# A hand-ordered attention-plus-FFN kernel: a new instruction order, new PSUM banks and a reshuffled head of loads

## The chip, the cores and the metric

The kernel runs on one core of a Trainium2 chip. The core has a matrix engine (PE, whose weight loads are profiled apart as PEld), a vector engine (DVE), a scalar engine (ACT), GpSimd (POOL) and a sync engine (SP). Each engine works through its own instruction stream strictly in order and waits on semaphores. Here POOL issues nearly all loads, SP issues the transposing DMAs and the stores, and all of these share the core's 16 DMA engines. The metric is device time in microseconds for one execution, as a median of several runs.

## The reference

What is computed, cut to its core: a linear attention with an exponential feature map, followed by a two-layer feed-forward network (FFN) with a squared ReLU.

```python
# q, k, v: (8, 8, 576, 64); w_phi: (64, 128); w_in: (512, 2048); w_out: (2048, 512)
def phi(x):
    proj = np.einsum('bhsd,df->bhsf', x, w_phi)
    proj = proj - np.max(np.abs(proj), axis=-1, keepdims=True)
    return np.concatenate([np.exp(proj), np.exp(-proj)], axis=-1)
q_p, k_p = (phi(q), phi(k))
kv = np.einsum('bhsf,bhsd->bhfd', k_p, v)
z = np.sum(k_p, axis=2)
num = np.einsum('bhsf,bhfd->bhsd', q_p, kv)
den = np.einsum('bhsf,bhf->bhs', q_p, z)[..., None] + 1e-06
attn = num / den                      # then (batch, seq, heads*64) -> x: (4608, 512)
h = np.maximum(x @ w_in, 0.0)
out = h * h @ w_out
```

## The kernel before

The eight batches are worked through one after another. The attention of batch b+1 is woven into the FFN of token chunk b, so that PE always has dense FFN matmuls between the small attention ones. A chunk is 512 tokens of one batch; the ninth chunk gathers the last 64 tokens of all eight batches (tile `xS`).

Nothing is scheduled while the program is built. A planner object (`Plan`) collects 1,680 numbered steps, each tied to one engine (some have an alternative engine). Then five tables at the end of the file decide everything. `ORDER` is the list of step numbers in the order in which they are emitted, and so the order on every engine, which `pin` fixes with explicit dependencies. `BASES` has one digit for each of 377 PSUM groups, its first bank (0 to 7); a group that takes a bank waits until the last users of that bank are done. `STATES` has one bit for each of 233 copy-like steps: its own engine or its alternative (DVE or ACT). `GATES` (lines 1061 to 1073) holds back each load of batches 2 and up until a given step is done. `FILL` names the PE steps ahead of which a number of dummy matmuls on the tile `warm` is put (line 961).

The steps and lines that the text below speaks of:

- Head, batch 0: steps 13 and 12 load parts of k (L249), 14 and 19 load q (L278), 26 loads k of batch 1. Txk and Txq (L320) transpose 128-token blocks on PE; Cxk and Cxq (L193 on DVE, L195 on ACT) copy them out of PSUM. Pk and Pq (L347, L491) project on w_phi, Mk and Mq (L386, L405, L498) take the maxima, and the exponentials are on ACT (L394, L411, L584). V (L428) scales v, KV (L462) and KVs (L450) build kv, NA and NB (L648, L599) multiply by it. SA (L660), rd (L670) and xo (L674, L618) finish the rows. Steps 119, 120, 126 and 127 turn the first rows round, and f1a 307 (L813) is the first FFN matmul group.
- From batch 2 on, k and q are transposed by DMA (Xxk and Xxq, L331, on SP's queue), for batch 2 as steps 373 and 374. From batch 1 on the finished rows xo are transposed by DMA into `xT` (Xx, L708): steps 266, 275, 284 and 293 for batch 1; 437, 446, 455 and 464 for batch 2. `xo` is a ring of three buffers, so xo 292 has to wait until Xx 266 has read its buffer. In batches 3 to 7 the features of q are also transposed by DMA (Xf, L548).
- FFN: F1 (L788; L799, L813 and L827 for the first chunk) needs all of a chunk's `xT`; relu (L765 on ACT, L767 on DVE) and sq (L774) make h; F2 (L882) and F2h (L846, the last tokens) multiply by w_out; ot (L193 or L195) copies the result out, and SP stores it.
- On POOL, 33, 34 and 35 load v of batch 1, 36 to 39 w_out, 22 to 25 w_in, and 355 to 358 the k of batch 2, of which 356 is gated by step 170 (Pq of batch 0).

Of the kernel before, what the change touches and what calls it, by code (L numbers as in the profile page):

```python
# [108 lines left out]
def kernel(  # L109
# [858 lines left out]
    2, 0, 1, 13, 14, 12, 8, 6, 7, 5, 3, 4, 11, 19, 40, 41, 9, 42, 46, 48, 10, 74, 66, 47, 75, 15, 67, 76, 45, 43, 18,  # L968
    68, 44, 77, 17, 71, 58, 88, 16, 90, 59, 70, 89, 26, 91, 27, 60, 78, 69, 92, 20, 49, 80, 81, 79, 28, 50, 61, 21,
    93, 51, 94, 30, 72, 52, 54, 98, 63, 57, 95, 22, 99, 64, 131, 65, 73, 53, 23, 55, 62, 83, 24, 156, 82, 132, 25,  # L970
    157, 29, 56, 133, 101, 38, 85, 128, 102, 84, 109, 86, 34, 212, 87, 110, 103, 213, 36, 111, 129, 214, 37, 112,
    104, 113, 105, 100, 215, 130, 33, 194, 158, 106, 195, 218, 108, 107, 216, 188, 219, 96, 114, 189, 121, 97, 115,
    134, 217, 122, 200, 206, 135, 116, 123, 207, 124, 159, 117, 125, 201, 136, 118, 126, 160, 190, 137, 127, 119,
    191, 120, 142, 161, 138, 145, 143, 220, 146, 307, 308, 221, 147, 139, 311, 312, 309, 144, 233, 162, 313, 303,
    140, 163, 304, 223, 148, 141, 164, 149, 322, 305, 222, 165, 310, 150, 166, 319, 323, 306, 151, 315, 314, 320,
    152, 196, 316, 198, 321, 167, 317, 153, 197, 325, 154, 199, 318, 328, 168, 326, 169, 155, 324, 170, 174, 329,
    208, 171, 356, 186, 175, 331, 330, 35, 187, 209, 176, 184, 39, 245, 332, 334, 246, 32, 185, 173, 177, 234, 31,
    172, 340, 335, 178, 361, 211, 327, 202, 359, 179, 203, 341, 477, 360, 210, 481, 365, 180, 181, 204, 357, 242,
    336, 346, 225, 243, 224, 355, 205, 485, 358, 247, 342, 347, 236, 363, 182, 267, 226, 276, 362, 268, 352, 183,
    235, 337, 269, 364, 227, 366, 192, 277, 489, 353, 549, 193, 338, 278, 237, 254, 238, 373, 255, 239, 490, 348,  # L980
    244, 248, 241, 258, 240, 249, 228, 259, 229, 230, 270, 260, 231, 374, 285, 333, 343, 271, 232, 339, 261, 344,
    272, 262, 495, 286, 263, 499, 250, 287, 264, 273, 265, 503, 274, 266, 354, 294, 251, 295, 507, 252, 275, 256,
    296, 279, 508, 513, 280, 253, 257, 551, 345, 288, 281, 547, 289, 349, 282, 556, 283, 290, 379, 350, 284, 375,
    553, 382, 517, 291, 376, 744, 531, 292, 377, 367, 381, 293, 297, 535, 370, 298, 378, 369, 380, 521, 552, 299,
    351, 422, 548, 387, 300, 423, 539, 389, 546, 525, 301, 557, 390, 371, 543, 526, 388, 554, 438, 544, 413, 550,
    482, 439, 414, 372, 486, 440, 563, 483, 416, 368, 424, 484, 383, 487, 429, 417, 747, 478, 430, 555, 564, 474,
    488, 431, 384, 740, 492, 475, 479, 476, 391, 504, 395, 392, 385, 500, 493, 404, 505, 518, 406, 501, 302, 494,
    396, 522, 386, 506, 502, 510, 397, 523, 527, 405, 565, 480, 415, 496, 394, 524, 519, 540, 497, 511, 393, 514,
    498, 398, 532, 491, 515, 407, 754, 545, 541, 516, 419, 559, 447, 533, 420, 399, 400, 749, 448, 401, 741, 534,
    408, 449, 582, 512, 739, 409, 403, 402, 410, 562, 583, 536, 411, 737, 421, 412, 432, 520, 585, 668, 561, 433,  # L990
    738, 537, 528, 418, 584, 742, 434, 672, 435, 748, 529, 436, 558, 574, 538, 437, 425, 456, 577, 542, 722, 746,
    426, 457, 560, 575, 726, 934, 428, 458, 441, 730, 442, 743, 576, 530, 443, 604, 444, 427, 734, 445, 607, 446,
    450, 605, 465, 676, 466, 755, 467, 451, 680, 606, 735, 452, 570, 681, 453, 566, 454, 704, 572, 567, 686, 608,
    609, 571, 568, 459, 569, 708, 745, 460, 573, 616, 461, 586, 455, 619, 690, 462, 463, 587, 468, 618, 712, 509,
    469, 464, 578, 617, 470, 580, 694, 620, 471, 472, 716, 581, 628, 579, 640, 631, 698, 736, 621, 589, 665, 630,
    756, 588, 683, 699, 629, 596, 666, 673, 595, 717, 677, 674, 682, 632, 667, 590, 678, 641, 591, 633, 592, 684,
    669, 593, 594, 935, 598, 701, 937, 670, 473, 597, 642, 687, 679, 931, 671, 675, 945, 610, 688, 695, 611, 643,
    689, 691, 752, 685, 696, 612, 943, 702, 705, 613, 692, 614, 750, 765, 703, 706, 599, 936, 652, 693, 600, 767,
    707, 723, 928, 697, 653, 768, 939, 719, 724, 932, 655, 766, 601, 720, 753, 713, 603, 938, 654, 602, 757, 769,
    714, 751, 758, 622, 645, 731, 658, 930, 623, 759, 859, 715, 933, 760, 732, 771, 624, 634, 656, 625, 709, 635,  # L1000
    626, 863, 710, 770, 644, 636, 727, 711, 877, 733, 728, 637, 638, 772, 867, 729, 718, 721, 700, 807, 725, 761,
    615, 881, 764, 885, 809, 639, 762, 871, 808, 947, 763, 889, 872, 646, 810, 895, 647, 890, 795, 773, 797, 627,
    648, 1128, 913, 649, 650, 929, 798, 899, 774, 651, 777, 917, 796, 786, 657, 811, 776, 659, 903, 660, 775, 921,
# [104 lines left out]
```

## Time and profile before

| what | us |
|---|---|
| median of 3 runs | 345.33 |
| lowest, highest | 344.21, 345.71 |
| the profiled execution, its own time | 346.37 |
| its span (first to last instruction) | 344.6 |
| lies around the span in that execution | 1.77 |

The page of the profile gives PE busy 97% of the span, DVE 78%, ACT 64% and POOL 28%. A busy PE counts a matmul from its start to its modelled end; these overlap, so a gap of PE shows only where it is longer than that overlap. Times in the rows that follow count from the start of the span. SPq and POOLq are the DMA queues that these engines issue. A row of a timeline has start, duration, engine, line, operation and tiles, how many instructions are merged, and in brackets the idle time ahead of it and what ended that.

### The profile page before, as it was taken

The numbers are of one execution on the slowest core, as the hardware profiler recorded it, in microseconds if no ns is written. First come the engines' busy times: TensorE is split into PE (matmuls) and PEld (weight loads), VectorE is DVE, ScalarE is ACT, GpSimd is POOL, SyncE is SP. The second block draws the span as 40 slices with busy tenths as digits, with TensorE's granted clock in tenths as the row PEclk, the third lists the DMA queues.
The fourth block names the chain that finished last, engine by engine and source line by source line (L and its number), as shares of the span: only waits on it lengthen the run. The fifth ranks groups of instructions, "written<-read, shape, count | busy, mean of one in ns | idle before, by whom it ended". The sixth has DMA issues, their size and how long they took to land.

```text
span 344.6 us, 8417 instructions
## 1 busy us (share of the span) xinstructions
PE 333.8 (97%) x3371; PEld 189.0 (55%) x3402; DVE 269.2 (78%) x490; ACT 221.6 (64%) x388; POOL 95.5 (28%) x143
## 2 busy tenths in 40 slices
PE   8999999799998999999999999999999999999995
PEld 7789776445554554545545554555555454444443
DVE  5999998799888798888869987798978748861540
ACT  5999996499898787577887896886376201111101
POOL 8760571952910480104604061330000000000000
PEclk9999999999999999999999999999999999999999
DMA  9999999999999999999999999999964631101115
GB/s 135 176 205 202 201 131 157 181 154 210 128 165 195 197 169 197 177 182 185 193 178 178 170 195 168 214 151 171 199 123 92 135 90 54 47 0 62 31 58 126
DMA packets 142935, 51.51 MB, mean 149 GB/s; under 512 B 111472, under 2 KB 138416, under 8 KB 142896
## 3 DMA queue, kind: packets, MB, share of 16 engines
q1 hardware_dynamic: 97488, 32.35, 51.8%
q0 software_dynamic: 44960, 18.23, 46.3%
q8 instruction: 26, 0.43, 0.6%
q10 hardware_dynamic: 448, 0.39, 0.4%
q14 instruction: 13, 0.11, 0.1%
HBM read 36.73 MB, written 9.44 MB: 134 GB/s over the span
## 4 chain that ended last, share of the span: by engine, by line
PE 86%; DVE 5%; DMA 5%; issue 2%; ACT 1%; POOL 1%; SPq 0%; DVEq 0%; POOLq 0%
PE psum L882 31%; PE psum L788 30%; PE psum L648 5%; PE psum L462 5%; PE psum L347 5%; DMA xT<-xo 3%; PE psum L827 2%; DMA kT<-xk 2%; DVE mk L405 2%; PE psum L813 1%; PE psum L799 1%; PE psum L569 1%; PE psum L846 1%; PE psum L320 1%; PE psum L450 1%
## 5 line engine op out<-in xcount | busy, mean ns | idle before, releaser
L882 PE MATMUL psum<-wout,h 128*128 128x512 bf16 x529 | 127.7, 379 | 1.7 <-issue 0.3
L788 PE MATMUL psum<-xT,win 128*128 128x512 bf16 x448 | 104.7, 379 | 1.0 <-DMA xT<-xo 1.0
L765 ACT ACTIVATE hr<-psum 128x512 bf16<-128x512 f32 x95 | 54.9, 601 | 47.9 <-DVE h L774 28.8
L882 PEld LDWEIGHTS <-h 128*128 128x128 bf16 x560 | 51.3, 98 | 56.7 <-issue 0.3
L788 PEld LDWEIGHTS <-win 128*128 128x128 bf16 x512 | 47.4, 98 | 53.6 <-DMA xT<-xo 1.4
L774 DVE TENSOR_TENSOR h<-hr 128x512 bf16<-128x512 bf16 x144 | 56.6, 415 | 10.6 <-ACT hr L765 10.2
L544 ACT ACTIVATE qf<-psum 128x1024 bf16<-128x1024 f32 (+1 forms) x50 | 45.6, 937 | 8.6 <-PE psum L347 6.1
L405 DVE TENSOR_REDUCE mk<-psum 128x8 f32<-128x1024 f32 (+1 forms) x38 | 42.3, 1119 | 4.0 <-ACT kn L411 1.9
L411 ACT ACTIVATE kn<-psum 128x1024 bf16<-128x1024 f32 (+1 forms) x38 | 36.0, 947 | 12.8 <-PE psum L347 11.1
L411 ACT ACTIVATE kp<-psum 128x1024 bf16<-128x1024 f32 (+1 forms) x38 | 35.6, 948 | 8.2 <-PE psum L347 6.6
L767 DVE TENSOR_SCALAR hr<-psum 128x512 bf16<-128x512 f32 x49 | 33.1, 684 | 9.0 <-PE psum L788 8.2
L660 DVE TENSOR_TENSOR psum<-psum,en 128x520 f32<-128x520 f32 (+1 forms) x39 | 27.2, 703 | 10.4 <-PE psum L648 6.1
L648 PEld LDWEIGHTS <-qpn 128*128 128x128 bf16 x624 | 27.0, 97 | 15.0 <-issue 3.3
L269 POOL DMA_DIRECT2D xq<-in_q_dram x24 | 17.3, 727 | 56.3 <-issue 14.0
L531 DVE TENSOR_REDUCE mq<-psum 128x8 f32<-128x1024 f32 (+1 forms) x25 | 27.8, 1113 | 6.5 <-PE psum L347 3.9
L648 PE MATMUL psum<-kv,qpn 128*128 128x65 bf16 x624 | 30.2, 193 | 1.9 <-DVE xo L674 1.7
L249 POOL DMA_DIRECT2D xk<-in_k_dram x27 | 19.9, 740 | 30.6 <-ACT en L508 15.3
L584 ACT ACTIVATE qpn<-psum 128x1024 bf16<-128x1024 f32 (+1 forms) x30 | 27.0, 956 | 1.8 <-PE psum L569 1.8
L674 DVE TENSOR_TENSOR xo<-psum,rden 128x512 bf16<-128x512 f32 (+1 forms) x39 | 26.3, 684 | 2.4 <-DMA xT<-xo 1.8
L195 ACT ACTIVATE ot<-psum 128x512 f32<-128x512 f32 x18 | 10.8, 598 | 25.7 <-PE psum L882 25.7
L249 POOL DMA_DIRECT2D xv<-in_v_dram x27 | 19.8, 740 | 14.6 <-PE psum L788 11.7
L428 DVE TENSOR_TENSOR va<-xv,va 128x1280 bf16<-128x1280 bf16 (+2 forms) x34 | 23.2, 710 | 0.0
(79 smaller groups left out, 352.8 us busy)
## 6 DMA issues: line engine op xcount, KB each, us to landing
out_dram<-ot SPq DMA_DIRECT2D x32, 256.0 KB, 3.0
xk<-in_k_dram POOLq DMA_DIRECT2D x25, 128.0 KB, 5.1
xq<-in_q_dram POOLq DMA_DIRECT2D x24, 128.0 KB, 5.1
xv<-in_v_dram POOLq DMA_DIRECT2D x24, 128.0 KB, 5.1
win<-in_moe_w_in_dram POOLq DMA_DIRECT2D x4, 512.0 KB, 10.7
wout<-in_moe_w_out_dram POOLq DMA_DIRECT2D x4, 512.0 KB, 15.5
xq<-in_q_dram POOLq DMA_DIRECT2D x4, 256.0 KB, 6.1
out_dram<-ot SPq DMA_DIRECT2D x6, 128.0 KB, 2.4
```

The source lines that it names most:

```text
L249: pin(nc.gpsimd.dma_start(out=x[:, m0 + a * 512 : m0 + z * 512].rearrange("p (h x) -> p h x", x=4 * D), in_=src[b][2 * a : 2 * z, 0:512, : ...
L405: pin(nc.vector.tensor_reduce(out=mk_view(g), in_=ps2(pj)[:, :, : n * Fd].rearrange("p e (i f) -> p e i f", f=Fd), axis=AX.X, op=ALU.max, ...
L411: pin(nc.scalar.activation(out=dst[slot][:, :, :n, :].rearrange("p e i f -> p e (i f)"), in_=ps2(pj)[:, :, : n * Fd], func=ACT.Exp, scale= ...
L531: pin(nc.vector.tensor_reduce(out=mqb[:, c, :, :n], in_=ps2(pj)[:, :, : n * Fd].rearrange("p e (i f) -> p e i f", f=Fd), axis=AX.X, op=ALU ...
L544: pin(nc.scalar.activation(out=o, in_=i_, func=ACT.Exp, scale=sgn))
L648: pin(nc.tensor.matmul(out=o[:, u // 4, u % 4 * D1 : (u % 4 + 1) * D1], lhsT=qpn[slot][:, sg * half + u * m : sg * half + u * m + P], rhs= ...
L660: pin(nc.vector.tensor_tensor(out=o, in0=o, in1=enb[:m, c, :].rearrange("t (b h) -> t b h", b=2).to_broadcast([m, 2, 4, D1]), op=ALU.mult))
L765: pin(nc.scalar.activation(out=hr[sl], in_=ps1(g), func=ACT.Relu))
L767: pin(nc.vector.tensor_scalar(out=hr[sl], in0=ps1(g), scalar1=0.0, scalar2=None, op0=ALU.max))
L774: pin(nc.vector.tensor_tensor(out=dst, in0=i_, in1=i_, op=ALU.mult))
L788: pin(nc.tensor.matmul(out=o, lhsT=win[mc // 4][:, kc, mc % 4 * P : (mc % 4 + 1) * P], rhs=x, start=(kc == 0), stop=(kc == KC - 1)))
L882: pin(nc.tensor.matmul(out=ps1(g), lhsT=h2[c % 2][mc // 4][:, mc % 4, tt * P : (tt + 1) * P], rhs=wout[mc // 4][:, mc % 4, :], start=(mc = ...
```

## The change

Four of the five tables are replaced; all functions and `GATES` stay. What that makes of each engine's stream, read off the two lists:

- SP: the same 113 instructions in the same order.
- POOL: the same 139; 15 positions differ, all among the first 29. From load 356 on the order is unchanged but for step 34. In the head, k (12) is issued ahead of q (14), and four small loads and the big load xq 30 change places. Of the weights, w_in is issued 23, 22, 24, 25 instead of 22, 23, 24, 25, and w_out 37, 38, 36 instead of 38, 36, 37. Step 34 (64 rows of v, batch 1) moves from between two w_out loads to behind the gated load 356.
- PE: the same 547 steps; 341 positions differ, most by one to three places, in the last quarter by up to 24. The steps that precede positions 66, 117, 121, 132, 198, 286, 320, 367 and 539 are the same set in both. The number of switches between 64-row and 128-row matmuls is 109 in both.
- DVE and ACT: 72 steps change engine; DVE goes from 490 to 480 steps, ACT from 391 to 401.
- Banks: 315 of the 377 groups get another one.
- Dummy matmuls: 127 in 9 places instead of 128 in 14.

```diff
 ORDER = [
-    2, 0, 1, 13, 14, 12, 8, 6, 7, 5, 3, 4, 11, 19, 40, 41, 9, 42, 46, 48, 10, 74, 66, 47, 75, 15, 67, 76, 45, 43, 18,
-    68, 44, 77, 17, 71, 58, 88, 16, 90, 59, 70, 89, 26, 91, 27, 60, 78, 69, 92, 20, 49, 80, 81, 79, 28, 50, 61, 21,
-    93, 51, 94, 30, 72, 52, 54, 98, 63, 57, 95, 22, 99, 64, 131, 65, 73, 53, 23, 55, 62, 83, 24, 156, 82, 132, 25,
...
-    553, 382, 517, 291, 376, 744, 531, 292, 377, 367, 381, 293, 297, 535, 370, 298, 378, 369, 380, 521, 552, 299,
...
-    426, 457, 560, 575, 726, 934, 428, 458, 441, 730, 442, 743, 576, 530, 443, 604, 444, 427, 734, 445, 607, 446,
...
-    469, 464, 578, 617, 470, 580, 694, 620, 471, 472, 716, 581, 628, 579, 640, 631, 698, 736, 621, 589, 665, 630,
...
+    2, 0, 1, 13, 12, 14, 7, 8, 6, 5, 3, 4, 11, 19, 40, 41, 9, 42, 47, 48, 10, 66, 74, 46, 67, 15, 75, 44, 68, 43, 18,
+    76, 71, 77, 17, 45, 16, 70, 88, 26, 58, 90, 78, 59, 28, 89, 91, 49, 21, 80, 69, 60, 50, 79, 20, 30, 61, 51, 94,
+    53, 98, 72, 95, 27, 57, 92, 63, 52, 23, 99, 73, 56, 22, 54, 64, 93, 62, 24, 82, 131, 25, 65, 86, 55, 156, 132,
...
+    375, 381, 517, 376, 744, 292, 531, 378, 367, 382, 293, 297, 370, 521, 298, 377, 369, 380, 535, 552, 299, 548,
...
+    575, 441, 726, 934, 458, 730, 442, 743, 576, 530, 443, 604, 444, 676, 445, 607, 542, 446, 465, 421, 605, 450,
...
+    578, 617, 717, 470, 690, 580, 620, 471, 694, 472, 587, 581, 640, 628, 579, 698, 631, 736, 677, 756, 629, 665,
...
 ]
 BASES = (
-    '1455230076225145762234566476424460160675235573406256700052456706030226636000051065454425544316464174'
+    '5212763076042032244453244556262426500440442663207220321070763220400000244524237610267776646734050067'
...
 )
 STATES = (
-    '0100000001011000110001110010000100000000100011110000100100001010000000101000100000000000001011010001'
+    '1101000000111000010001100011000000000000000000100100011100000011000000001000100100000100001001100010'
...
 )
...
 FILL = {
-    40: (0, 26), 42: (0, 11), 74: (0, 5), 76: (0, 7), 58: (0, 10), 60: (4, 16), 92: (4, 1), 51: (6, 9), 131: (4, 8),
-    156: (3, 2), 101: (3, 23), 188: (4, 3), 134: (2, 1), 142: (5, 6),
+    40: (0, 26), 42: (0, 11), 66: (0, 5), 68: (3, 7), 88: (3, 23), 49: (1, 10), 51: (3, 12), 131: (2, 28),
+    145: (3, 5),
 }
```

10 lines of the change are left out of this document (5 added, 5 removed), and 148 rows, old and new, of the table ORDER.

## The prediction

> **What bounds the kernel now.** I read the page first, then what PE waited for, then the windows, and last the timeline of the queues behind each wait. The first two:
>
> ```profile
> PE 333.8 (97%) x3371; PEld 189.0 (55%) x3402; DVE 269.2 (78%) x490; ACT 221.6 (64%) x388; POOL 95.5 (28%) x143
> ...
> PE psum L648 <- DVE xo L674: 1.7, 1, 1.7
> ...
> PE psum L788 <- DMA xT<-xo: 1.0, 1, 1.0
> PE psum L347 <- DMA kT<-xk: 0.4, 1, 0.4
> ```
>
> PE is the bound, and of its visible waits after the head there are three: 1.7 us for a vector result, 1.0 and 0.4 us for transposing DMAs. The windows cut at those places (span in us, then busy time of each engine) say where the rest is:
>
> ```profile
> 4.00:26.00 22.00, 20.92 (x363) 17.27 (x363) 20.48 (x42) 19.82 (x39) 16.61 (x24) 1.00 1.49 188
> 26.00:61.00 35.00, 34.84 (x537) 26.64 (x539) 32.43 (x63) 29.68 (x55) 13.58 (x21) 1.00 1.32 174
> 61.00:71.00 10.00, 8.12 (x73) 4.15 (x75) 7.22 (x12) 6.03 (x9) 8.97 (x14) 1.00 1.50 174
> 71.00:109.00 38.00, 37.69 (x395) 19.86 (x398) 33.64 (x56) 34.70 (x58) 14.81 (x22) 1.00 1.22 170
> 111.00:187.00 76.00, 75.52 (x730) 39.70 (x736) 63.76 (x112) 57.48 (x100) 25.69 (x38) 1.00 1.24 185
> 188.50:337.40 148.90, 148.11 (x1198) 75.27 (x1212) 106.61 (x200) 68.81 (x122) 12.93 (x19) 1.00 0.66 117
> ```
>
> From 71 us on PE is idle 0.31 us in 38.00, 0.48 in 76.00 and 0.79 in 148.90. Nothing that a better order could take away is left there beyond the two DMA waits. The slack is all ahead of 71 us: 1.9 us between 61 and 71, and in the head, where DVE (20.48 of 22.00) and ACT (19.82) are the bound and PE fills its gaps with dummies. So the question is what fixes 71 us. The queues answer it (SP's issues, the rows for L249 and L708 with their times to landing, PE and the chain):
>
> ```profile
> 36.48 0.70 POOL L249 DMA_DIRECT2D xk<-in_k_dram  x1 [10.32 <-PE psum L569]
> ...
> L249 POOL DMA_DIRECT2D xk<-in_k_dram x2: 703/708/712, 46.0 to 46.8; - x2
> ...
> DMA to landing us min/median/max: 3.0/3.0/3.1
> ...
> 49.91 4.33 SPq L331 DMA_TRANSPOSE kT<-xk  x1
> 54.54 4.74 SPq L331 DMA_TRANSPOSE qT<-xq  x1
> 59.33 6.61 SPq L708 DMA_TRANSPOSE xT<-xo  x4
> ...
> 59.33 4.60 DMA xT<-xo
> ...
> 64.02 0.70 DVE xo L674
> ...
> L708 SPq DMA_TRANSPOSE xT<-xo x4: 1192/1265/1282, 59.3 to 64.7; - x4
> ...
> DMA to landing us min/median/max: 4.6/5.5/6.1
> ...
> 70.86 1.47 PE L788 MATMUL psum<-xT,win 128*128 128x512 bf16 x6
> ```
>
> The last k load of batch 2 is issued at 46.8 and lands 3.0 to 3.1 us later, at 49.8. SP issues Xxk 373 at 49.91 and Xxq 374 behind it, 4.33 and 4.74 us each. Only then, at 59.33, does Xx 266 go out; it lands at 63.93. That frees the ring buffer of xo 292 (64.02), on which PE's NA 297 waits for its bank, and SP can issue Xx 293 (64.7), which lands up to 6.1 us later, at 70.8. The first F1 of the next chunk starts at 70.86. So 71 us is set by a chain of loads and transposes, and PE has about 1.8 us of slack ahead of it (10.00 - 8.12). The loads themselves run at the rate of the DMA engines (window 26 to 50):
>
> ```profile
> GB/s 207 224 193 185 183 194 213 198 203 196 199 202 229 194 200 207 212 208 199 200 198 197 225 182 179 196 205 207 197 177 178 152 88 129 101 28 78 186 178 81
> ```
>
> At a steady 200 GB/s until about 45 us, the landing at 49.8 follows from the bytes queued ahead of it.
>
> **The change part by part.** *Up to 70.86.* SP's order is the same, POOL's from load 356 on too but for step 34, and the bytes ahead of load 358 are the same. NA 297 again takes a bank that xo 292 has to free, and the PE steps ahead of F1 (position 132) are the same set. So 70.86 stays, and the stall of 1.7 us stays: 0.0 us. What hides the edits of the head is that stall; how much of it they use, from these rows:
>
> ```profile
> 0.99 2.95 PE L961 MATMUL psum<-warm 128*128 128x128 bf16 x26 [0.99 <-DVE warm L235]
> ...
> 7.74 0.73 PE L961 MATMUL psum<-warm 128*128 128x128 bf16 x10
> ...
> 15.25 1.46 PE L961 MATMUL psum<-warm 128*128 128x128 bf16 x23
> ...
> 9.00 0.41 DVE L193 COPY kT<-psum 128x512 bf16<-128x512 bf16 x1
> ...
> 11.12 0.28 DVE L193 COPY kT<-psum 128x256 bf16<-128x256 bf16 x1
> ```
>
> Txk 58 now stands behind 23 dummies and one Txq instead of 10 dummies: 13 more dummies at 63 ns (1.46 us over 23) and four matmuls of the like, about 1.0 us later. Its copy on DVE (9.00) follows it, and DVE, which has no idle time there, loses that. Cxk 50 (0.28) leaves DVE, Cxk 207 (0.41) comes to it; 93 and 95 change places, at 0.41 each. In sum the head ends 1.0 - 0.28 + 0.41 = 1.1 us later at most. At the other end it ends 0.3 us earlier, if DVE would have waited there anyway. I take 0.6, inside the cover of 1.8; without the cover it would cost its whole length, as nothing between 26 and 61 us (PE idle 0.16) could catch it up. Step 34 behind gated load 356 adds one POOL issue, about 0.65 us by its like among the small loads (the row below), ahead of the k loads. POOL waits for room in the DMA queue there anyway, so I take 0.0; up to 0.65 if it did not.
>
> ```profile
> 37.17 0.65 POOL L257 DMA_DIRECT2D xv<-in_v_dram  x1
> ...
> 42.60 0.61 POOL L257 DMA_DIRECT2D xk<-in_k_dram  x1 [1.08 <-DMA xv<-in_v_dram]
> ```
>
> *The wait for chunk 2 (109 to 111).*
>
> ```profile
> 92.33 0.68 DVE L498 TENSOR_REDUCE mq<-psum 128x4 f32<-128x512 f32 x1
> 93.06 1.23 DVE L405 TENSOR_REDUCE mk<-psum 128x8 f32<-128x1024 f32 x1
> 94.41 0.71 DVE L660 TENSOR_TENSOR psum<-psum,en 128x520 f32<-128x520 f32 x1
> ...
> 95.86 0.69 DVE L674 TENSOR_TENSOR xo<-psum,rden 128x512 bf16<-128x512 f32 x1
> ...
> 98.42 3.38 SPq L331 DMA_TRANSPOSE kT<-xk  x1
> ...
> 106.08 4.66 DMA xT<-xo
> ...
> 110.79 3.19 PE L788 MATMUL psum<-xT,win 128*128 128x512 bf16 x14 [0.95 <-DMA xT<-xo]
> ```
>
> Xx 464, issued at 106.08, lands at 110.74; PE has been waiting for 0.95 us by then. SP issues without a pause from Xx 446, right behind xo 445 (95.86 to 96.55), through Xxk 755 (98.42) to there, so an earlier xo 445 moves the landing by as much. In the new order NA 441 stands one F2 earlier (four matmuls, 0.9 us by 3.19 for 14). Its product SA (94.41) still follows Mk 575 on DVE, which ends at 94.29, so SA wins the little between 94.29 and 94.41, and what follows no longer waits for PE; about 0.3 us in all at xo 445. Bounds: 0 (DVE decides) and the whole 0.95 us of the wait. I take -0.3, as DVE's row is the nearest.
>
> *The wait for Xxk 1137 (187.8).*
>
> ```profile
> 187.81 0.29 PE L347 MATMUL psum<-wphi,kT 64*128 64x128 bf16 x4 [0.39 <-DMA kT<-xk]
> 187.93 0.39 PE L347 MATMUL psum<-wphi,qT 64*128 64x128 bf16 x8
> ```
>
> Pq 1022 (eight matmuls) now runs ahead of Pk 1139 and fills about 0.1 to 0.2 of the 0.39. I take -0.2; bounds 0 and -0.39.
>
> *New waits.* With 315 banks changed, 72 steps on another engine and PE order shuffled by one to three places, some operand will come later than its turn. One that I can place: NA 610 moves ahead of two F1s while its kv copy (593) goes from DVE to ACT behind a relu, and by ACT's durations there (0.60 for a relu, 0.40 for a kv copy, rows below) it would be ready 0.1 to 0.3 us after PE. The trace before has such small waits too (0.31 + 0.48 + 0.79 us, above). Bounds: -0.5, if the new banks remove half of those, and +1.6, if they double. I take +0.4, near the one case that I can price.
>
> ```profile
> 114.02 0.60 ACT L765 ACTIVATE hr<-psum 128x512 bf16<-128x512 f32 x1 [1.39 <-PE psum L788]
> ...
> 115.32 0.40 ACT L195 ACTIVATE kv<-psum 128x260 bf16<-128x260 f32 x1
> ```
>
> *Engines' load and mode switches.* Ten steps net go from DVE to ACT; behind PE, 0. The switches between 64-row and 128-row matmuls are 109 in both: 0. After 111 us, and at the end, the sets of PE steps are the same at each point where `xT` is needed: 0.
>
> **Sum.** 0.0 - 0.3 - 0.2 + 0.4 = -0.1 us on a span of 344.6. The profiled execution took 346.37 in all; the runs' median is 345.33. The forecast is 345.33 - 0.1 = **345.2 us**: no change that can be told. What this measurement can tell from no change is about 0.5%, 1.7 us.
>
> **The rivals.** *The head outruns its cover (slower).* Place: the first 26 us. If the dummies and the moved copies delay f1a 307 by more than 1.8 us, NA 297 comes after xo 292. The gate of load 356 (step 170, at 36.48) slips as well, and with it the loads and transposes up to 70.86. Every further microsecond is then lost whole, since PE is full afterwards. For: DVE and ACT have no slack there and the new order starts with a delay of 1.0 us. Against: my worst sum is 1.1. A slip of 4 us would give 345.2 + 2.2 = 347.4 us.
>
> *The clock (slower).* Between Fq 131 and KVs 109 the new order has no dummies, where the old one had 2 and 23 (15.25, 1.46 us). The granted clock is 1.00 in all windows above, and a dummy takes 63 ns there; the first 26 took 2.95 us, 113 ns each. If PE fell back to that pace for as long again, with the head's worst sum: 2.95 + 1.1 - 1.8 = 2.2 us, 347.4 us. [...] But Pq 156, Pq 128 and Fq 101 still run in that stretch, and no quiet piece of it should reach 2 us. No trace here shows a fall.
>
> *The chain to 70.86 gets shorter (faster).* The search may have won what I can't see: loads landing sooner through the new order of the head, worth up to the 1.7 us stall, plus both later waits (1.0 + 0.4). All of it would give 342.2, half of it 343.7; I take 342.9. For: that stall is the largest there is. Against: the bytes and SP's order are unchanged.
>
> *Many small waits (slower).* PE, DVE and ACT are all at 88% or more between 71 and 109 (37.69, 33.64 and 34.70 of 38.00). If new waits add up to over 1.8 us, the time is about 347.3.
>
> **How the numbers follow.** Forecast 0.61; shorter chain 0.14; head 0.11; clock 0.04; small waits 0.10. The forecast's own range is 344.2 to 346.4 (its bounds: -0.95 - 0.39 + 0.3, and +1.1). To hold the time 8 times in 10 the range takes in half of the shorter chain and most of the slower cases: 343.4 to 347.5. Faster by over 0.5% (below 343.6): 0.14. Slower by over 0.5% (above 347.06): 0.25, the three slower cases together. Within: 0.61.
>
> **What would show it.** In the profile after, the chain of waits should again have a transposing DMA from about 59.3, an xo at about 64.0 and the first L788 at about 70.9; the wait L648 <- xo should still be there, shorter by the head's slip. The L788 wait near 110 should be about 0.7 us and the one at 188 about 0.2. A first L788 well off 70.9 would make the chain theory wrong; a PE idle time over 3 us between 71 and 337, or a granted clock under 1.00 ahead of 60 us, the forecast.

## The result: 0.8% slower, and the profile after

Over 20 executions each the changed kernel took 348.24 us (345.87 to 354.98) and the kernel before 345.25 (344.08 to 346.95): ratio 1.0080, 95% interval 1.0059 to 1.0101, 3.0 us more. The ratio and its interval leave out three of the changed kernel's 20 executions, slow ones more than 1.5% above its fastest; the medians count all 20. The forecast was 345.2, its range 343.4 to 347.5; the median lies above it. The profiled execution took 349.26 us, its span is 347.5.

The line of all engines on the page after, then what PE waited for (total us, times, longest):

```profile
PE 335.3 (96%) x3372; PEld 190.0 (55%) x3401; DVE 264.9 (76%) x480; ACT 225.9 (65%) x398; POOL 95.6 (28%) x143
```

```profile
PE psum L450 <- ACT qpn L584: 1.1, 1, 1.1
...
PE psum L648 <- DMA qpn<-qf: 0.7, 1, 0.7
...
PE psum L347 <- DMA kT<-xk: 0.6, 1, 0.6
PE psum L788 <- DMA xT<-xo: 0.5, 1, 0.5
PE psum L788 <- ACT qf L544: 0.5, 1, 0.5
...
PE psum L648 <- DVE xo L674: 0.3, 1, 0.3
```

The waits that the old kernel had (L648 for xo 1.7, L788 for xT 1.0) have shrunk to 0.3 and 0.5, as a later PE must make them. New are L648 for qpn and L788 for ACT. The windows at the cuts that the prediction used (span in us, busy time of PE, PEld, DVE, ACT, POOL, then PE's clock, DMA share, GB/s):

```profile
4.00:26.00 22.00, 19.48 (x331) 16.61 (x331) 18.61 (x34) 17.94 (x36) 16.27 (x23) 0.92 1.44 176
26.00:61.00 35.00, 34.41 (x520) 25.95 (x523) 31.79 (x66) 31.19 (x57) 12.07 (x18) 1.00 1.30 168
61.00:71.00 10.00, 9.63 (x109) 5.69 (x108) 7.96 (x14) 5.85 (x9) 8.82 (x13) 1.00 1.66 161
...
111.00:187.00 76.00, 73.82 (x721) 38.77 (x726) 62.04 (x107) 58.38 (x103) 24.68 (x37) 1.00 1.24 185
...
15.10:18.51 3.41, 2.26 (x28) 1.44 (x26) 3.34 (x7) 3.41 (x8) 2.40 (x4) 1.00 1.66 156
18.51:21.92 3.41, 3.16 (x57) 2.97 (x58) 2.58 (x6) 2.50 (x6) 3.41 (x5) 0.50 1.24 184
```

The first of the two short stretches in the kernel before:

```profile
15.10:18.51 3.41, 3.39 (x60) 2.64 (x57) 3.41 (x7) 3.41 (x6) 1.48 (x3) 1.00 1.80 179
```

Two things differ here. In the head PE's granted clock is 0.50 for 3.41 us from 18.51 on, right behind 3.41 us in which PE was busy for 2.26 (3.39 in the kernel before). And between 111 and 187 us PE is idle for 76.00 - 73.82 = 2.18 us, where it was 0.48.

How the loss builds up is read best from PE's lag: the start (of the first weight load) of PE's next step once both kernels have run the same set of PE steps (132, 236, 286 and 342 of 547), minus that start in the kernel before (70.86, 133.23, 164.01 and 198.43 us). For the changed kernel it is +2.98 at 62.7 us, +1.57 at 71, +1.03 at 133, +2.58 at 164 and +2.87 at 198. From there it stays level to the last step (+2.86). So the head's slip is mostly given back, and 1.8 us come anew between 133 and 198. In this execution they come at three places: 0.9 at NA 646 (from 1.03 to 1.92), 0.7 at F1 882 (to 2.58), and 0.3 at Pk 1139, where the lag first falls to 2.12, as the old kernel waits there too, and then rises to 2.87. Two rows of PE in the head and at 71 us belong to the slip: a wait for a k load, and the first F1 (L788).

```profile
11.16 0.27 PE L320 MATMUL psum<-ident,xk 128*128 128x128 bf16 x2 [0.64 <-DMA xk<-in_k_dram]
...
72.43 0.82 PE L788 MATMUL psum<-xT,win 128*128 128x512 bf16 x3
```

The chain of waits of the changed kernel names what they are (start, us, what):

```profile
128.37 9.33 DMA qpn<-qf
137.70 0.04 issue
137.75 0.42 PE psum L648 x8
...
147.17 4.76 DMA qpn<-qf
151.93 0.02 issue
...
152.01 1.02 ACT qf L544
...
153.13 0.92 ACT qf L544
154.06 0.04 issue
154.10 2.10 PE psum L788 x9
...
182.47 8.37 DMA kT<-xk
190.84 0.04 issue
190.88 0.29 PE psum L347 x4
```

At each of the three places a transposing DMA ends the wait: Xf 644 lands at 137.70 and PE's NA 646 starts 0.05 us later; Xf 799 lands at 151.93, and only then can ACT's Eqn 822 and Eqp 821 free the bank that F1 882 needs; Xxk 1137 lands at 190.84 and Pk 1139 starts 0.04 later. PE's rows at the first place, before and after, and the time from issue to landing of Xf 644 in the kernel before (row of its line, issued at 127.3):

```profile
134.54 2.32 PE L882 MATMUL psum<-wout,h 128*128 128x512 bf16 x10
136.70 0.41 PE L648 MATMUL psum<-kv,qpn 128*128 128x65 bf16 x8
```

```profile
134.72 2.32 PE L882 MATMUL psum<-wout,h 128*128 128x512 bf16 x10
137.75 0.42 PE L648 MATMUL psum<-kv,qpn 128*128 128x65 bf16 x8 [0.71 <-DMA qpn<-qf]
```

```profile
DMA to landing us min/median/max: 9.0/9.0/9.0
```

In the old kernel Xf 644 lands at 136.3; NA 646 reads it at 136.7, with no wait and 0.4 us of margin. In the new order NA 646 stands one F2 (889) earlier, and the margin is gone.

### The profile page after: what moved, and what is told of

It is laid out like the page before. It is cut to its first block, busy times and chain, and to the rows that moved or that the text cites. A ratio compares the mean times of both kernels' runs of the same rounds, so it can differ in the third digit from the quotient of the medians.

```text
span 347.5 us, 8423 instructions
## 1 busy us (share of the span) xinstructions
PE 335.3 (96%) x3372; PEld 190.0 (55%) x3401; DVE 264.9 (76%) x480; ACT 225.9 (65%) x398; POOL 95.6 (28%) x143
## 4 chain that ended last, share of the span: by engine, by line
PE 79%; DMA 11%; ACT 5%; issue 2%; POOL 1%; DVE 1%; SPq 0%; DVEq 0%; POOLq 0%; ACTq 0%
PE psum L882 29%; PE psum L788 28%; PE psum L648 5%; PE psum L462 5%; PE psum L347 4%; DMA qpn<-qf 4%; DMA xT<-xo 3%; DMA kT<-xk 2%; PE psum L827 2%; DMA xk<-in_k_dram 2%; ACT kn L411 1%; ACT qf L544 1%; PE psum L569 1%; ACT kp L411 1%; PE psum L846 1%
## 5 line engine op out<-in xcount | busy, mean ns | idle before, releaser
L882 PE MATMUL psum<-wout,h 128*128 128x512 bf16 x531 | 126.3, 379 | 1.7 <-issue 0.5
L788 PE MATMUL psum<-xT,win 128*128 128x512 bf16 x448 | 105.6, 379 | 1.0 <-DMA xT<-xo 0.5
L765 ACT ACTIVATE hr<-psum 128x512 bf16<-128x512 f32 x98 | 57.2, 598 | 45.9 <-PE psum L788 24.7
L788 PEld LDWEIGHTS <-win 128*128 128x128 bf16 x512 | 47.1, 98 | 53.6 <-issue 1.0
L767 DVE TENSOR_SCALAR hr<-psum 128x512 bf16<-128x512 f32 x46 | 31.2, 687 | 14.4 <-PE psum L788 12.6
L195 ACT ACTIVATE ot<-psum 128x512 f32<-128x512 f32 x21 | 12.3, 597 | 41.4 <-PE psum L882 41.0
L648 PEld LDWEIGHTS <-qpn 128*128 128x128 bf16 x624 | 27.1, 98 | 14.8 <-issue 1.8
L648 PE MATMUL psum<-kv,qpn 128*128 128x65 bf16 x624 | 30.3, 193 | 1.2 <-DMA qpn<-qf 0.7
L249 POOL DMA_DIRECT2D xv<-in_v_dram x27 | 19.6, 734 | 18.6 <-PE psum L648 11.7
```

Of the source, the lines that this page charges most:

```text
L249: pin(nc.gpsimd.dma_start(out=x[:, m0 + a * 512 : m0 + z * 512].rearrange("p (h x) -> p h x", x=4 * D), in_=src[b][2 * a : 2 * z, 0:512, : ...
L648: pin(nc.tensor.matmul(out=o[:, u // 4, u % 4 * D1 : (u % 4 + 1) * D1], lhsT=qpn[slot][:, sg * half + u * m : sg * half + u * m + P], rhs= ...
L765: pin(nc.scalar.activation(out=hr[sl], in_=ps1(g), func=ACT.Relu))
L767: pin(nc.vector.tensor_scalar(out=hr[sl], in0=ps1(g), scalar1=0.0, scalar2=None, op0=ALU.max))
L788: pin(nc.tensor.matmul(out=o, lhsT=win[mc // 4][:, kc, mc % 4 * P : (mc % 4 + 1) * P], rhs=x, start=(kc == 0), stop=(kc == KC - 1)))
L882: pin(nc.tensor.matmul(out=ps1(g), lhsT=h2[c % 2][mc // 4][:, mc % 4, tt * P : (tt + 1) * P], rhs=wout[mc // 4][:, mc % 4, :], start=(mc = ...
```

## Experiments

All ratios are to the kernel before, run on the same chip. "Lag" is PE's lag in the run's profiled execution, one for each run. In some of these executions PE's clock fell to 0.50, which is part of their lag: in the change (18.5 us), before_fewer_dummies (18.2), new_until_112 (18.6 and 127.8), before_late_readers (65.6), after_xf644_first (18.8 and 158.7), before_dma_order (69.4 and 130.9) and before_later_loads (142.0).

| run | ratio (95%) | lag at 71 | 133 | 164 | 198 us |
|---|---|---|---|---|---|
| the change | 1.0080 (1.0059-1.0101) | +1.57 | +1.03 | +2.58 | +2.87 |
| after_dummies | 1.0058 (1.0027-1.0089) | +0.40 | +0.03 | +1.55 | +1.11 |
| before_fewer_dummies | 1.0036 (1.0006-1.0066) | +0.44 | -0.30 | -0.31 | +0.81 |
| after_earlier_load | 1.0071 (1.0039-1.0104) | +0.41 | +0.52 | +2.85 | +2.95 |
| old_until_71 | 1.0046 (1.0007-1.0086) | -0.27 | -0.35 | +2.17 | +3.04 |
| old_until_115 | 1.0073 (1.0039-1.0107) | -0.64 | +1.11 | +1.79 | +2.36 |
| new_until_112 | none (see below) | +1.04 | +4.31 | +4.31 | +3.86 |
| new_115_to_192 | 1.0087 (1.0053-1.0121) | +0.02 | +2.21 | +3.39 | +4.06 |
| new_135_to_164 | 1.0078 (1.0048-1.0107) | -1.28 | +0.12 | +3.55 | +3.24 |
| old_until_164 | 1.0009 (0.9977-1.0042) | -2.21 | -1.40 | -1.40 | -0.29 |
| before_early_readers | 1.0040 (1.0008-1.0071) | -0.38 | +0.12 | +1.03 | +0.58 |
| before_late_readers | 0.9996 (0.9961-1.0030) | +1.83 | +1.33 | +1.66 | +1.42 |
| after_late_readers | 1.0041 (1.0003-1.0079) | +0.50 | -0.01 | +1.62 | +1.39 |
| after_late_readers_2 | 1.0083 (1.0045-1.0120) | +0.74 | -0.31 | +1.77 | +1.54 |
| after_late_readers_3 | 1.0151 (1.0096-1.0206) | +1.34 | +0.68 | +3.76 | +3.72 |
| new_115_to_192_late | 1.0090 (1.0055-1.0125) | +0.59 | +1.90 | +3.81 | +3.94 |
| after_xf644_first | 1.0118 (1.0055-1.0181) | +3.63 | +3.44 | +8.98 | +8.53 |
| before_dma_order | 1.0215 (1.0173-1.0256) | +2.66 | +12.84 | +12.84 | +12.38 |
| before_later_loads | 1.0256 (1.0179-1.0334) | +0.43 | +1.03 | +9.15 | +8.70 |

**The clock.** Dummies put back, and taken out of the old kernel:

```diff
 FILL = {        # after_dummies, against the changed kernel
+    156: (6, 5), 101: (4, 16),
 FILL = {        # before_fewer_dummies, against the kernel before
-    156: (3, 2), 101: (3, 23),
```

> The changed kernel with 21 dummies put back in the stretch where the old one had 25: 5 ahead of Pq 156 and 16 ahead of Fq 101, in banks that are free there. In the changed kernel's trace PE was busy 2.26 of the 3.41 us up to 18.51 and then ran at a granted clock of 0.50 for 3.41 us. If that quiet stretch makes the clock fall, and the fall is most of the loss, the clock stays at 1.00 in 4 to 26 us, f1a 307 comes about 1.5 us earlier (near 27.5 instead of 28.95), and the time drops by about 1.5 us against the changed kernel, to a ratio of 1.002 to 1.005 to the kernel before. If the head's order (a later Txk 58, the loads behind it) and the new waits after 111 us make the loss and the clock is only beside it, the ratio stays near 1.008 though the clock stays at 1.00. If the clock falls for another reason, it is 0.50 again somewhere ahead of 26 us.

> The kernel before without its 2 dummies ahead of Pq 156 and its 23 ahead of Fq 101, nothing else changed. If PE's quiet stretch of some 3.4 us makes the clock fall, PE is busy about 2 of the 3.5 us between 15 and 18.5, and a stretch of 3.4 us at a granted clock of 0.50 follows, in some runs or all. The old head has 1.8 us of slack at 61 to 71 us, so a fall worth 1.5 to 2 us of PE's time there would cost the whole kernel little by slack alone (0 to 0.3 us, 345.3 to 345.6). But if load 356, which waits for Pq 170, slips with it, and the last k load lands later by as much, the time rises by 1 to 2 us (ratio 1.003 to 1.006). If the dummies do nothing there, the clock stays at 1.00 and the ratio is 0.999 to 1.001.

The window of the head, after_dummies and then before_fewer_dummies:

```profile
4.00:26.00 22.00, 21.13 (x363) 17.65 (x363) 18.89 (x37) 18.32 (x37) 16.27 (x23) 1.00 1.47 184
```

```profile
4.00:26.00 22.00, 18.30 (x306) 15.05 (x306) 18.68 (x34) 17.75 (x36) 16.80 (x24) 0.92 1.46 183
```

In the head the dummies held the clock. Taken out of the old kernel, they left a mean clock of 0.988 to 0.995 in 11 of 12 executions; in the kernel before, run beside it, it was below 0.998 in 5 of 35. (One fall of 3.41 us to 0.50 takes 0.005 off the mean; where it fell is seen in profiled executions alone.) In the changed kernel the mean was 0.995 or less in 9 of 20 executions (median 349.26 us), and the other 11 have a median of 347.68. That is still 2.4 us above the kernel before, so the clock is the smaller part of the loss. With the dummies back, the mean was 0.995 or less in 3 of 12, the head's lag at 62.7 us is 2.23 in place of 2.98, and at 71 us 0.40 in place of 1.57. The time gains less: 1.0058 against 1.0080, with intervals that overlap.

**The late load.**

```diff
 GATES = {
-    356: 170,
+    356: 167,
```

> The changed kernel with load 356 let go after Tx 167 in place of Pq 170, so that it is issued at about 36.5 us as in the kernel before and not at 39.06. Theory of the head: PE's slip of 2.6 us at 38.5 costs time because it lets the load wait, the DMA engines run dry, and the last k load lands at 51.88 in place of 49.83; with the load let go in time the landing is back near 49.8 to 50.3, the first F1 of the next chunk starts at 71.0 to 71.6 instead of 72.43, and the time falls by 0.8 to 1.5 us (ratio 1.004 to 1.006). Rival, PE itself is late: NA 297 came at 65.69 against 62.72, and its product feeds the last transposes; then the landing moves but F1 stays at 72.0 to 72.4, and the ratio stays at 1.007 to 1.008.

The load was issued at 36.31 and the last k load landed at 50.10 in place of 51.88, and F1 came at 71.3. But the clock did not fall in that execution, and in after_dummies, with the landing as late as 51.73, F1 has the same lag. So the late load cost nothing that can be seen; the ratio of 1.0071 agrees.

**Which stretch.** Mixtures of the two orders, each with its own banks, engines and dummies:

```
 # old_until_71:   old ahead of step 482, new from there
 # old_until_115:  old ahead of step 669, new from there
 # new_115_to_192: new only from step 669 to step 992
 # new_135_to_164: new only from step 889 to step 1068
 # old_until_164:  old ahead of step 1068, new from there
 # new_until_112:  new ahead of step 677, old from there
```

> All steps that the kernel before runs ahead of PE's F1 482 (the first 71 us) in its order, with its banks, engines and dummies; from there on those of the changed kernel. Theory of the head alone: all 3.0 us come from the first 71 us, and the time is that of before, ratio 0.999 to 1.001. Theory of head and new waits: the first 71 us are worth 1.0 to 1.2 us behind the wait at 110 us, and the waits at 136, 152 and 189 us (0.87, 0.66 and 0.75) stay: the time is 346.8 to 347.3, ratio 1.004 to 1.006.

> All steps that the kernel before runs ahead of PE's F1 669 (its first 115 us) as in that kernel, with its banks, engines and dummies; the rest as in the changed kernel. Theory of the new waits behind 111 us: NA 646 waits again for the transposing DMA Xf 644 near 135 us, F1 882 for its bank near 152, Pk 1139 for Xxk 1137 near 189, and the ratio is 1.004 to 1.006. Theory of the head (everything before 111 us): ratio 0.999 to 1.001.

> The opposite half: all steps that the changed kernel runs ahead of PE's F1 677 (its first 112 us) as there, the rest as in the kernel before. Theory of the new waits behind 111 us: none of them is there, only the head's loss of about 1.0 us behind the wait at 110 (more in runs with the halved clock): ratio 1.002 to 1.004. Theory of the head: the ratio of the changed kernel, 1.007 to 1.009.

> The kernel before with the changed kernel's order, banks and engines only in the stretch between PE's F1 669 and NA 992 (115 to 192 us); what is ahead of it and behind it is as before. Theory of the new waits: this stretch alone carries the loss that old_until_115 showed (1.0073): ratio 1.004 to 1.007. Rival, the tail behind 192 us carries it: ratio 0.999 to 1.002.

> The kernel before with the changed kernel's order, banks and engines only between PE's F2 889 and F2 1068 (about 135 to 164 us in its trace): there NA 646, F1 882 and NA 825 wait for the landing of Xf 644, for the bank that ACT frees behind Xf 799, and for Xf 823. From the delays of old_until_71 against the kernel before (-0.35 us at 133, +2.17 at 164, +2.48 at 172, +1.72 at 188, +3.03 at 193): if the delays are made where they appear, this stretch alone costs 1.5 to 2.5 us, ratio 1.004 to 1.007. Rival, they come from the order ahead of 135 or go away again behind 164: ratio 0.999 to 1.002.

> The kernel before up to PE's F2 1068 (164 us), the changed kernel from there on. Pq 1022 then runs ahead of Pk 1139, but three F1s that stood behind it in the kernel before stand ahead, and Pk 1139 still waits for Xxk 1137 near 188 to 190. By the same delays this part costs 0.3 us at 172, and 0 to 0.9 at 190: ratio 1.000 to 1.003. Rival, the loss is made in the second half of the stretch: ratio 1.005 or more.

With the old head and no fall of the clock, old_until_71 is 0.35 us ahead at 133 and still ends 3.03 behind. Its lag is made in the stretch, at the same place (chain of waits of old_until_71):

```profile
127.00 10.46 DMA qpn<-qf
137.46 0.04 issue
137.51 0.42 PE psum L648 x8
```

NA 646 starts at 137.51, against 137.75 in the changed kernel, though PE was 1.4 us less late at 133: the landing decides, and in these two executions the head's lead or lag is lost at it. The new order in 135 to 164 us alone brings 1.0078, its seam included, and the new order behind 164 no loss that can be told from the times (1.0009), though in the profiled execution PE's lead shrank there from 1.4 to 0.3 us. The window 135 to 165, before, changed kernel, new_135_to_164 and old_until_164:

```profile
135.00:165.00 30.00, 29.89 (x307) 15.96 (x307) 26.42 (x48) 21.10 (x40) 5.69 (x9) 1.00 1.14 181
```

```profile
135.00:165.00 30.00, 28.63 (x287) 15.11 (x287) 22.81 (x39) 21.11 (x39) 5.63 (x8) 1.00 1.09 188
```

```profile
135.00:165.00 30.00, 27.10 (x270) 14.30 (x269) 21.10 (x36) 20.48 (x38) 5.63 (x8) 1.00 1.02 174
```

```profile
135.00:165.00 30.00, 29.48 (x325) 15.94 (x324) 25.92 (x49) 20.38 (x39) 6.55 (x10) 1.00 1.09 175
```

PE's idle time there: 0.11, 1.37, 2.90 and 0.52 us. Of the 2.90, two bank waits of 0.7 us each belong to the seam of the mixture, where ACT's old order meets the new banks:

```profile
PE psum L788 <- ACT qf L544: 1.0, 1, 1.0
...
PE psum L648 <- ACT kp L411: 0.7, 1, 0.7
PE psum L882 <- ACT qf L544: 0.7, 1, 0.7
```

So 1.0078 is too much by up to 1.4 us (0.4%), which leaves about half of it or more to the stretch. The wait of 1.0 us for ACT behind Xf 799 is the changed kernel's own. new_135_to_164 differs from the kernel before in 34 positions of PE, 31 banks and the engine of 8 steps, all at once; which of these costs what was not separated, but for the two readers below. old_until_115 and new_115_to_192 have a seam too: NA 610 waits 0.7 us there for its kv copy. new_until_112 took 351.89 us (median of 6, against 346.17) and decides nothing: PE waited 2.1 us at about 126 us, in the old order behind the seam, where Xf 632 landed 10.4 us after its issue.

**Moving the readers.** First the old kernel with two readers one step earlier, as the change has them:

```diff
 ORDER = [       # before_early_readers: PE's steps
-    F2 871, F2 889, NA 646, F2 895   ...   F1 892, F1 922, NA 825
+    F2 871, NA 646, F2 889, F2 895   ...   F1 892, NA 825, F1 922
```

> The kernel before with two readers moved one step ahead, as the change has them: NA 646, which waits for the transpose Xf 644 (landing at 136.33 us), ahead of F2 889, and NA 825, which waits for Xf 823 (160.73), ahead of F1 922. In its trace they come 0.16 and 0.24 us behind the landings, and the step that they pass is 0.86 us long. Theory of the early readers: PE waits 0.5 to 0.9 us at 136 and up to 0.6 at 160, the time rises by 0.7 to 1.3 us, ratio 1.002 to 1.004, and the profile shows L648 waiting for qpn<-qf at both places. Rival: the landings come sooner or the loss is made good by less waiting further on: ratio 0.998 to 1.001.

NA 825 waited as foretold: Xf 823, issued at 154.81 and landed 6.5 us later at 161.30, then PE. NA 646 had luck: Xf 644 landed at 136.15, and the lag rose there only from 0.12 to 0.37. NA 825 cost 0.66 us of lag (0.37 just ahead of it, 1.03 behind).

```profile
159.83 1.03 PE L788 MATMUL psum<-xT,win 128*128 128x512 bf16 x4
161.34 0.42 PE L648 MATMUL psum<-kv,qpn 128*128 128x65 bf16 x8 [0.49 <-DVE h L774]
```

(The row names a vector result that ends at 161.32; NA 825 doesn't read it.) Then the mend:

```diff
 ORDER = [       # after_late_readers, with after_dummies' FILL
-    F2 885, NA 646, F2 895, F2 889, NB 648   ...   Pk 1139, KVs 972, F1 1095, KV 973, KV 974
+    F2 885, F2 895, F2 889, NA 646, NB 648   ...   KVs 972, F1 1095, KV 973, KV 974, Pk 1139
-    Eqn 822, en 824, Eqp 821, relu 865, Eqp 833   ...   F1 882, F1 874, F1 886
+    Eqp 833, Eqn 822, en 824, Eqp 821, relu 865   ...   F1 886, F1 882, F1 874
                 # after_late_readers_2: Pk 773, Pq 795, F2 899 ahead of NB 648
                 # after_late_readers_3: also F1 922, NA 813, Pq 843 ahead of NA 825, SA 814 of SA 826, NB 815, F1 910 of NB 827; F1 896, F1 900 ahead of F1 882
                 # new_115_to_192_late: as _2, in new_115_to_192, and F1 669 ahead of NA 610
                 # before_late_readers: F2 895 ahead of NA 646, Pk 1139 behind KV 974, store 509 behind store 545
```

> The changed kernel with the 21 dummies put back (as in after_dummies) and the three readers of late transposes moved back, nothing moved on SP: F2 895 and F2 889 stand ahead of NA 646, which waits for Xf 644; Pk 1139, which waits for Xxk 1137, stands behind KVs 972, F1 1095, KV 973 and KV 974; Eqp 833 on ACT stands ahead of Eqn 822, which waits for Xf 799, and F1 886 ahead of F1 882. Theory of the new waits: the gaps of PE near 136, 152 and 189 us (0.87, 0.66 and 0.75 us in the changed kernel, 1.10, 0.40 and 0 in after_dummies) fall to 0.2 us or less each and the ratio from 1.0058 to 1.001 to 1.003. Rival, the loss is not in these waits or comes back as a wait behind them: the ratio stays at 1.005 to 1.007.

> after_late_readers with one fault of it mended: there NB 648 stood right behind NA 646 and waited 0.8 us for the vector result in between (SA 647); now Pk 773, Pq 795 and F2 899 stand between them. The rest as in after_late_readers. Theory of the new waits: the gap at 137.6 (0.96 us) falls to 0.2 or less, only the wait at 110 us (0.74) is left behind 71 us, and the ratio goes from 1.0041 to 1.000 to 1.002. Rival, part of the loss is elsewhere: 1.004 or more.

> after_late_readers_2 with the two waits mended that its trace still has in the stretch: at 160.45 us (1.28 us) NA 825 waits for the transposing DMA Xf 823; now F1 922, NA 813 and Pq 843 stand ahead of it (and SA 814 ahead of SA 826 on DVE, NB 815 and F1 910 ahead of NB 827). At 151.7 us (0.78 us) F1 882 waits for a bank that ACT frees behind the transpose Xf 799; now F1 896 and F1 900 stand ahead of it. In after_late_readers_2 PE was level with the kernel before up to 158 us and 1.5 us behind it at 192. Theory that the stretch costs by readers that stand too early for their transposes, five of them and not three: PE stays within 0.5 us of the kernel before up to 192 us and the ratio is 1.000 to 1.003. Rival, waits only move on along the chain of transposes (each NB lets the next Xf go): 1 us or more is lost again by 192 us, ratio 1.004 or more.

> new_115_to_192 (1.0087) with the readers moved back as in after_late_readers_2, and F1 669 ahead of NA 610, which in that mixture waited 0.84 us for its kv copy at 118. Theory of the new waits: the gaps at 118, 136, 153 and 190 us fall to 0.2 each or less and the ratio to 0.999 to 1.002. Rival, the stretch costs by other things than these waits: the ratio stays at 1.005 or more.

> The kernel before with the same kind of edit, meant to make it faster: F2 895 ahead of NA 646; Pk 1139 behind Pq 1022, KVs 972, KV 973 and KV 974, so that the wait for Xxk 1137 (0.39 us, 1.66 us in before_fewer_dummies) is filled; and the output store 509, ready at 58.55 us but standing on SP right ahead of Xx 464 (0.66 us from its start to that of Xx 464), moved to behind store 545 near 84 us, where SP is idle. If a reader's wait costs its length: 0.4 to 0.6 us less at 188 us and up to 0.6 us less at 110 us, ratio 0.997 to 0.999. Rival: landing times follow from the loads in flight and not from SP's order, and PE finds another wait: ratio 0.999 to 1.002.

No mend paid (after_late_readers, 1.0041, can't be told from after_dummies, 1.0058), and my theory that the loss is gone once the readers stand later fell. The waits that I moved away did go, but others came: NB 648 for the vector result SA 647 (0.80 us), then NA 825 for Xf 823 (1.1), then two waits for ACT's relus (0.9 and 1.1). In before_late_readers the wait for Xxk 1137 is gone and the time the same. In the three after_late_readers runs each wait that was moved away was followed by another.

**Moving DMAs.**

```diff
 ORDER = [       # after_xf644_first: SP
-    Xf 656, Xf 644
+    Xf 644, Xf 656
                 # before_dma_order: SP; on POOL load 744 behind load 368
-    Xxq 374, Xx 266, Xx 275   ...   Xf 656, Xf 644   ...   Xxk 755, Xf 608, Xx 455, st 509, Xx 464   ...   Xf 1002, Xxk 1137
+    Xx 266, Xx 275, Xxq 374   ...   Xf 644, Xf 656   ...   Xf 608, Xx 455, st 509, Xx 464, Xxk 755   ...   Xxk 1137, Xf 1002
                 # before_later_loads: loads 935, 937, 931, 945, 752, 943, 750, 936 behind F1 723
 GATES = {
-    935: 641,
+    935: 723,
```

> The changed kernel with one step of SP moved: the transposing DMA Xf 644, whose inputs are there at 120.05 us, goes out ahead of Xf 656, behind which it stood until 128.37, so it lands 7 us or more before NA 646 reads it. If the wait of NA 646 (0.87 us in the trace of the changed kernel) costs its length, it is gone and the time falls by 0.5 to 0.9 us, ratio 1.005 to 1.006. If the time is set by another chain behind it (F1 882's bank, Xxk 1137), the wait is gone and those waits grow by as much: ratio still 1.007 to 1.009.

> The kernel before with PE's, DVE's and ACT's order, its banks and dummies as they are, and only steps of the DMA queues moved: on SP Xxq 374 behind Xx 266 and Xx 275, Xxk 755 behind Xx 464, Xf 644 ahead of Xf 656, Xxk 1137 ahead of Xf 1002; on POOL the load xqr 744, which waits for Xxq 374, behind load 368. Theory that the order of SP's transposes sets PE's waits: Xx 266 goes out near 55.8 in place of 59.33, Xx 464 near 104.5 in place of 106.08, Xxk 1137 near 178.4 in place of 181.19; the waits of 1.7, 1.0 and 0.4 us shrink to a third or less and the time falls by 1.5 to 3 us, ratio 0.991 to 0.996. Rival: the transposes that were moved back, or the loads that wait for them, come too late in their turn, or the landing times follow from the bytes in flight and not from the order; then the ratio is 0.998 or more.

> The kernel before with the run of loads that begins with 935 (116.94 us in its trace) held back until PE's F1 723 (near 122.4), nothing else changed. It asks why the same transposing DMA took from 2 to 14 us. If transposes are slow because loads are in flight beside them: Xf 632, issued at 115.45 and landed at 121.95 (6.5 us) in the kernel before, lands within 4 us of its issue, as Xf 620 did (2 us at 111), and Xf 644, issued at 127.3, now lands later than 9.0 us after its issue, so NA 646 waits 1 us or more at 136. If the time of a transpose follows from the transposes queued on SP, Xf 632 takes 6 us or more again.

I expected gains of up to 3 us from the first two and got losses (1.0118 and 1.0215). before_dma_order's chain has one transpose (Xf 632) that took 14 us, and PE stood still for 7.8 us behind it:

```profile
119.63 14.04 DMA qpn<-qf
133.66 0.02 issue
133.68 0.02 ACTq L544
```

In the kernel before that transpose took 6.5 us, beside the loads that POOL begins to issue at 116.94. What POOL's loads moved while Xf 632 was under way (queue of POOL's loads: packets, MB, share of the 16 DMA engines; the kernel before, new_until_112, before_dma_order):

```profile
q0 software_dynamic: 358, 0.18, 30.7%
```

```profile
q0 software_dynamic: 1528, 0.64, 67.4%
```

```profile
q0 software_dynamic: 1918, 0.83, 67.3%
```

It took 6.5, 10.4 and 14.0 us there. In eight of the 20 profiles these loads moved 0.01 MB or less meanwhile, and it took 4.4 to 4.5 us in each; in ten they moved 0.16 to 0.39 MB, and it took 6.1 to 7.2. Holding the loads back until 125.5 (before_later_loads) also gave 4.5 us, but that alone shows nothing: seven profiles without that gate have 4.5 us too, three of them (before_early_readers, new_135_to_164, old_until_164) with PE's and SP's order of the kernel before up to there. So one code can draw 4.5 or 6.5. Held back, the loads met Xf 644, which took 12.5 us beside 0.90 MB in place of 9.0 beside 0.39 (row of L548 in before_later_loads, then the PE row):

```profile
DMA to landing us min/median/max: 5.9/9.2/12.5
```

```profile
140.87 0.42 PE L648 MATMUL psum<-kv,qpn 128*128 128x65 bf16 x8 [2.98 <-DMA qpn<-qf]
```

So in these profiles a transpose landed late where loads moved much data beside it (Xf 632: 4.5 us beside 0.01 MB or less, 14.0 beside 0.83). Two of the waits of the change fit this: Xf 644 took 9.3 us beside 0.47 MB there (10.5 beside 0.59 in old_until_71), and Xxk 1137 took 8.4 beside 0.57, against 6.6 beside 0.37 in the kernel before. The two runs that moved transposes or loads in the old kernel lost more (1.0215 and 1.0256) than any order of PE here.

## Why the prediction was wrong, point by point

- *New waits, +0.4: the step that failed.* The mechanism was named, the size was wrong. Of the 1.84 us by which PE's lag grew between 133 and 198, 1.55 are new waits (0.89 at NA 646, 0.66 at F1 882) in place of 0.4, just under my bound of +1.6. I priced one case, NA 610 behind its kv copy, and that one cost nothing: the copy ended at 117.64, ahead of NA 610 at 117.89. What I left out were the readers of SP's transposes. The old trace has PE's weight loads of NA 646 and NA 825 only 0.16 and 0.24 us behind the landings, and moving a reader ahead of one F2 (0.86 us) could be read from the two orders. The rival "many small waits" was this mechanism, at 0.10; its 347.3 us was too low by 0.9. The forecast's own range, 344.2 to 346.4, also left my bound out: 345.33 + 1.6 is 346.9.
- *Up to 70.86, 0.0: the second term that failed.* F1 came at 72.43, 1.57 us late, and 1.03 of that was left at 133. "The head ends 1.1 us later at most, I take 0.6": without the clock's fall it was 2.2 us at 62.7 us (after_dummies), so the cover of 1.8 was outrun by 0.4, the lag of that run at 71. I had left out the k load that Txk 49 reads: PE waited 0.64 us for it at 11.16. The price that I gave to a slip past the cover, all of it lost, was not borne out: a third of it was back by 133, most of that at the wait near 110, and in old_until_71 a lead of 0.35 in its place made no difference behind NA 646.
- *The clock, 0.04.* By the mean clock it fell in 9 of 20 executions. I argued that no quiet piece would reach 2 us; none did (the longest wait is 1.1), and the clock fell. That pieces so short keep the clock was my estimate; no trace had shown it. "No trace here shows a fall" holds up to PE's last matmul in the kernel before (340.9 us); behind it that trace has a clock of 0.50 from 343.0 on. What differed at the fall is the busy share of the 3.41 us ahead of it: 66% here and 99% in the kernel before, where 25 dummies of 63 ns were 1.6 us of it.
- *Step 34 and load 356, 0.0.* Right in effect: the load came 2.6 us later, and moving it back changed nothing that can be told. The old trace has POOL waiting there until an xv load had landed (1.08 us ahead of 42.60); that it waited for room in the queue was my reading, which no row shows.
- *The wait for chunk 2, -0.3.* Right: the lag falls by 0.4 there (1.45 to 1.04).
- *The wait for Xxk 1137, -0.2.* Wrong: Pq 1022 fills its place, but Xxk 1137 landed 8.37 us after its issue in place of 6.6, and the lag, which falls from 2.58 to 2.12 ahead of it, grew to 2.87: +0.3 in all. That this is the new order's doing is not shown. In before_fewer_dummies, which has the old order there, PE waited 1.5 us for Xxk 1137, and the lag grew by 1.1 between 164 and 198.
- *What would show it.* All three signs that I had named against the chain or the forecast came: the first L788 off 70.9, a granted clock below 1.00 ahead of 60 us, and PE idle for 4.0 us between 71 and 337 (266.0 less 262.0 busy). The last was a weak sign, as the kernel before already has 2.9.

In the profiled execution the terms add up: 1.45 from the head at 109 us, less 0.42 at chunk 2, 1.55 of new waits and 0.29 at Xxk 1137 are 2.87. How they share the 3.0 us of the medians is not settled: the lag that the stretch adds varies from execution to execution (+1.1 to +3.4 in the six other profiles with its PE order unmended), each mend made waits of its own, and the banks and engines of the stretch were never changed apart from its order.

## What to carry to other kernels

A landing time in one trace is one draw (Xf 632 took 4.5 or 6.5 us in the same code): look first, in any new order, at who reads a DMA, what was moved from ahead of it, and which loads move data beside it. A margin of the size of the landing's spread might do for a reader (an estimate of 1.5 to 3 us here, from 9.0 to 10.5 us of Xf 644 and 4.4 to 7.2 of Xf 632), but no mend here showed that it pays. To find where a reordered kernel loses, compare the starts at points where both have run the same set of steps, and then mix the two orders at such points; a mixture makes waits at its seam, which have to be taken off. Dummy matmuls that look like idle filling may hold the clock: without 25 of them the mean clock here was 0.988 to 0.995 in 11 of 12 executions.

## What the runs showed of the hardware

- The clock halved for 3.41 us, from 18.51 to 21.92, without a long wait ahead of it. PE was busy for 2.26 us (66%) of the stretch of the same length before it, with no wait over 1.1 us; with 3.39 us busy in the same stretch, the kernel before kept 1.00. Seven more falls, in before_fewer_dummies, new_until_112, after_xf644_first and before_dma_order, followed a stretch of 3.41 us with PE busy for 0 to 59%. But the share alone does not decide: in after_xf644_first stretches with 46% (66.5 to 70.0 us) and 64% (138.2 to 141.6) brought no fall.
- The transposing DMA Xf 632 took 4.4 to 4.5 us from issue to landing with POOL's loads moving 0.01 MB or less meanwhile (eight profiles), 6.1 to 7.2 with 0.16 to 0.39 MB (ten), 10.4 with 0.64 and 14.0 with 0.83. A longer transfer also meets more bytes, so the steps in between are no price list; the gap between the first two groups, with no load or some load, is the finding.
- The same code up to 71 us brought PE there 2.2 us earlier (old_until_164) and 1.8 later (before_late_readers, whose clock fell at 65.6 us) than in the kernel before. The small effects above stand against that spread.
